# A gated MLP and long convolution, forward and backward: gate and up with rows on the partitions, h turned by TensorE, gradients turned by DMA in the last phase

## Chip, cores, metric

One Trainium2 chip, one core used. The metric is device time of one execution in microseconds (us). Profiled executions are single executions, whose span ("span") is a little shorter than the time of the same execution as timed.

TensorE does the matmuls, VectorE the elementwise products, ScalarE the copies out of PSUM (the memory that matmuls write to) and part of the DMA issuing, GpSimd and SyncE the rest of the issuing. In the lines of the profile these are PE, DVE, ACT, POOL and SP; PEld is the weight load of TensorE, to "turn" is to transpose, and SPq and ACTq are the issuing queues of SyncE and ScalarE.

## The reference

S = 2048 rows, D = 1024 columns, F = 3584 hidden columns, all bfloat16. The kernel computes the output and nine gradients; there is none for `B_x`, which is not used.

```python
# ... fft convolution _A_ref(q, k, v, shift_k, ssm_k, ssm_D), which multiplies q by a
# long convolution of (shifted k) * v along the rows ...
def _B_ref(x, w_gate, w_up, w_down):
    g = jnp.einsum("bsd,df->bsf", x, w_gate)
    u = jnp.einsum("bsd,df->bsf", x, w_up)
    h = g * u
    return jnp.einsum("bsf,fd->bsd", h, w_down)

x  = A_q
xn = _layernorm(x, axis=-1)
s  = _A_ref(xn, A_k, A_v, A_shift_k, A_ssm_k, A_ssm_D)
g  = _silu(_B_ref(xn, B_w_gate, B_w_up, B_w_down))
out = x + s * g
# outputs: out, and jax.vjp of it applied to grad_out
```

## The kernel before

It runs in six stages one after the other on TensorE. The convolution's forward and backward are cut into small steps, which `pump` and `bpump` hand out between matmuls in step with TensorE's progress. So VectorE, which does most of the convolution, is filled from TensorE's side.

| stage | what TensorE computes | what runs beside it |
|---|---|---|
| start | turns of the first normalized rows | layer norm |
| gate and up | g and u, 14 slabs of 256 hidden columns | rest of layer norm, forward convolution |
| down projection | h x w_down, then gating | gating on VectorE |
| backward | gradient of h, then those of w_gate and w_up | backward convolution |
| gradient of w_down | h^T x gradient | end of the backward convolution |
| gradient of x | gradients of g and u x weights^T | layer norm backward, gradient of the filter |

The gradients of g and u are needed twice, in two forms. The weight gradients contract over rows, so rows must be on the partitions. The gradient of x contracts over hidden columns, so those must be. The kernel before computes g and u, and with them their gradients, with hidden columns on the partitions; for the weight gradients it then turns them on TensorE.

```python
    def gu_unit(fc, s0, ns, w, tick):                      # before: hidden columns on partitions
        ...
            for a in range(2):
                ps = ps_gu.tile([P, 512], F32, name="psg")
                for dc in range(DC):
                    nc.tensor.matmul(ps[:, 0:n], w[:, dc, a, fi * P:(fi + 1) * P], XNT[q][:, dc, qo:qo + n],
                                     start=(dc == 0), stop=(dc == DC - 1))
                nc.scalar.copy(out=gut[:, a, o:o + n], in_=ps[:, 0:n])
                flush(2)
                tick()
        sta(GUTd[fc, :, :, s0:s0 + ns], gut[:, :, 0:ns])
        ...
        tt(hT[:, 0:ns], gut[:, 0, 0:ns], gut[:, 1, 0:ns], MUL)
        st(HTd[...], hT[:, 0:ns])
```

`defer` puts a piece of TensorE work aside, and `flush(2)` lets it out after two more blocks, so that it doesn't stand in TensorE's order right behind what it needs. `ld`, `st` and `sta` are DMA issued by SyncE, GpSimd and ScalarE. The backward stage:

```python
    ps_b = pool("ps_b", 3, space=PSUM)
    ps_tr = pool("ps_tr3", 2, space=PSUM)
    ...
    BT = NSL * (8 + 16) + 84.0                             # the convolution is spread over so many steps

    def dh_half(fc, hf, wdt, dgu):
        gut = bg.tile([P, 2, 1024], BF16, name="gul", bufs=4)
        ld(gut[:], GUTd[fc, :, :, hf * 1024:(hf + 1) * 1024])
        dht = bg.tile([P, 1024], BF16, name="dht")         # 2 buffers
        for k in range(2):
            ...                                            # 8 matmuls of 512 columns: gradient of h
            nc.scalar.copy(out=dht[:, k * 512:(k + 1) * 512], in_=ps[:])
            flush(2)
            btick(1)
        dgt = gut
        with tc.high_priority(60):
            tt(dgt[:], gut[:], dht[:].unsqueeze(1).to_broadcast([P, 2, 1024]), MUL)

        def turn():
            sta(DGUTd[4 * hf:4 * hf + 4, :, :, fc, :].rearrange("b f a s -> f a b s"),
                dgt[:].rearrange("f a (b s) -> f a b s", s=256))
            for a in range(2):
                ps = ps_tr.tile([P, 8, P], BF16, name="tr")
                for i in range(8):
                    nc.tensor.transpose(ps[:, i, :], dgt[:, a, i * P:(i + 1) * P], ident[:])
                nc.scalar.copy(out=dgu[:, :, a, fi * P:(fi + 1) * P], in_=ps[:])
        defer(turn)
```

In the last stage, each 256 rows' gradients are loaded in the turned form that `DGUTd` holds, by two plain loads.

## Time and profile before

| | before |
|---|---|
| median of 3 runs | 2100.8 us (2099.44 to 2109.26) |
| profiled span | 2094.6 us, mean granted TensorE clock 0.996 |

The stages by the first matmul of each (the prediction cuts where source lines change, so its bounds differ by some 2 us and its lengths by up to 4 us):

| stage (us) | start | first slabs | gate and up | down projection | backward | gradient of w_down | gradient of x |
|---|---|---|---|---|---|---|---|
| begins at | 0 | 25.6 | 96.2 | 565.4 | 767.9 | 1467.0 | 1671.4 |
| length | 25.6 | 70.6 | 469.2 | 202.5 | 699.1 | 204.4 | 423.2 |
| TensorE busy | 8.9 | 66.5 | 453.3 | 199.3 | 675.8 | 202.4 | 411.7 |

Read a column as length less busy: that is what TensorE waited in the stage. Almost everything is busy, so a stage is as long as the work in TensorE's order, unless another engine is late. The lines of the profile that carry this are shown in the prediction.

### The profile page before, as it was taken

The page shows a single profiled execution, that of the slowest core. Times are in us where ns is not written, and L with a number is a line of the kernel's source. Part 1 is how long each engine was busy: PE and PEld are TensorE (multiplying, and loading weights), DVE is VectorE, ACT ScalarE, POOL GpSimd, SP SyncE. Part 2 cuts the span into 40 slices and gives each one's busy share as a digit, 9 for nine tenths or more (in the row PEclk, how much of TensorE's full clock was granted, in tenths as well). Part 3 has the DMA queues.
Part 4 walks back from the last instruction along what each step waited for, and adds up shares of the span by engine and source line. Part 5 has one row for each costly group of instructions (what it writes and reads, how often), then busy time and mean ns, then how long its engine had stood idle before and what let it go on. Part 6 is the DMA issues. An engine that isn't in the chain of part 4 may idle for free.

```text
span 2094.6 us, 28045 instructions
## 1 busy us (share of the span) xinstructions
PE 2017.9 (96%) x11036; PEld 1032.2 (49%) x11242; DVE 1451.0 (69%) x1950; ACT 677.2 (32%) x1028; POOL 301.4 (14%) x448
## 2 busy tenths in 40 slices
PE   6999999999999999999999999999999999999998
PEld 4455555556444445555444454554444444444443
DVE  7789898978555557776999877987885025344432
ACT  4633343334233343444333343433122102111111
POOL 3211111110011120001021112111111101110100
PEclk9999999999999999999999999999999999999999
DMA  8675665566597876667787777756955995444431
GB/s 266 206 249 193 211 224 200 170 217 216 191 335 238 251 268 225 209 195 197 246 254 235 217 228 230 227 186 197 258 157 148 244 293 180 149 152 162 149 103 41
DMA packets 412789, 435.51 MB, mean 208 GB/s; under 512 B 178176, under 2 KB 326952, under 8 KB 401648
## 3 DMA queue, kind: packets, MB, share of 16 engines
q1 hardware_dynamic: 260816, 184.84, 31.1%
q0 software_dynamic: 40768, 174.40, 24.1%
q10 hardware_dynamic: 111072, 74.47, 11.5%
q8 instruction: 88, 1.44, 0.3%
q14 instruction: 45, 0.37, 0.0%
HBM read 221.78 MB, written 179.34 MB: 192 GB/s over the span
## 4 chain that ended last, share of the span: by engine, by line
PE 36%; DVE 13%; issue 10%; DMA 3%; POOL 1%; ACT 1%; ACTq 0%; another core or an unknown queue 0%; DVEq 0%; POOLq 0%; SPq 0%
PE psx L1203 18%; PE psb L1170 9%; PE psb L1077 5%; DVE m L196 4%; DVE W L196 4%; DMA B<-HFd 2%; PE psdk L927 1%; DVE A L196 1%; DVE gul L196 1%; DVE B L196 1%; PE psb L1054 1%; PE psY L892 1%; DMA DGUTd<-gul 1%; DMA gul<-GUTd 0%; DMA B<-KFd 0%
## 5 line engine op out<-in xcount | busy, mean ns | idle before, releaser
L565 PE MATMUL psg<-U,wslab 128*128 128x512 bf16 (+1 forms) x1804 | 399.7, 374 | 7.6 <-DVE U L539 3.0
L1077 PE MATMUL psb<-U,U 128*128 128x512 bf16 x1741 | 395.3, 379 | 2.7
L1203 PE MATMUL psx<-U,dgut 128*128 128x512 bf16 x1380 | 306.7, 379 | 1.4
L1203 PEld LDWEIGHTS <-dgut 128*128 128x128 bf16 x1792 | 175.3, 98 | 211.4
L565 PEld LDWEIGHTS <-wslab 128*128 128x128 bf16 x1856 | 182.6, 99 | 195.1 <-issue 4.5
L1077 PEld LDWEIGHTS <-U 128*128 128x128 bf16 x1792 | 174.0, 98 | 194.1
L1054 PE MATMUL psb<-U,wdt 128*128 128x512 bf16 x872 | 204.4, 382 | 2.5 <-ACT bm L967 1.1
L1170 PE MATMUL psb<-U,U 128*128 128x512 bf16 x875 | 195.6, 379 | 2.0 <-DMA U<-HTd 0.9
L567 ACT CAST gut<-psg 128x512 bf16<-128x512 f32 x192 | 112.5, 587 | 221.4 <-PE psg L565 210.7
L952 PE MATMUL psbm<-U,ht 128*128 128x512 bf16 x766 | 170.2, 379 | 0.9
L1081 ACT CAST wb<-psb 128x512 bf16<-128x512 f32 x112 | 65.7, 587 | 268.5 <-PE psb L1077 231.5
L196 DVE TENSOR_TENSOR m<-A,B 128x1024 bf16<-128x1024 bf16 (+1 forms) x160 | 116.6, 792 | 43.0 <-DMA B<-KFd 17.6
L196 DVE TENSOR_TENSOR W<-W 128x1024 f32<-128x1024 f32 (+1 forms) x144 | 139.4, 985 | 2.9
L1170 PEld LDWEIGHTS <-U 128*128 128x128 bf16 x896 | 86.8, 98 | 102.1 <-DMA U<-HTd 1.4
L1054 PEld LDWEIGHTS <-wdt 128*128 128x128 bf16 x896 | 87.2, 99 | 95.4 <-issue 4.2
L1226 ACT ACTIVATE dx_t<-dxn 128x1024 bf16<-128x1024 f32 (+1 forms) x17 | 17.1, 1007 | 345.3 <-DVE dxn L196 283.9
L952 PEld LDWEIGHTS <-ht 128*128 128x128 bf16 x784 | 76.1, 98 | 89.0
L196 DVE TENSOR_TENSOR dka<-dkh,Wbc 128x1024 bf16<-128x1024 bf16 x16 | 11.1, 691 | 155.8 <-DMA dkh<-DKSHd 155.8
L1070 ACT COPY U<-tr 128x1024 bf16<-128x1024 bf16 x112 | 109.4, 1022 | 13.9 <-DMA gul<-GUTd 7.8
L1056 ACT CAST dht<-psb 128x512 bf16<-128x512 f32 x112 | 65.4, 588 | 121.9 <-PE psb L1054 77.2
L196 DVE TENSOR_TENSOR gul<-gul,dht 128x2048 bf16<-128x2048 bf16 x56 | 69.5, 1241 | 28.6 <-ACT dht L1056 28.2
L1203 PE MATMUL psx<-W,dgut 128*128 128x512 bf16 x376 | 85.6, 379 | 0.5
(240 smaller groups left out, 2428.5 us busy)
## 6 DMA issues: line engine op xcount, KB each, us to landing
gul<-GUTd SPq DMA_DIRECT2D x56, 512.0 KB, 5.9
DGUTd<-gul ACTq DMA_DIRECT2D x56, 512.0 KB, 7.7
dgut<-DGUTd SPq DMA_DIRECT2D x16, 1792.0 KB, 8.4
GUTd<-gut ACTq DMA_DIRECT2D x48, 512.0 KB, 4.3
A<-DYFd POOLq DMA_DIRECT2D x16, 1024.0 KB, 5.6
out_dram<-wb ACTq DMA_DIRECT2D x224, 64.0 KB, 2.6
ht<-HTd SPq DMA_DIRECT2D x7, 1536.0 KB, 8.0
KFd<-KX POOLq DMA_DIRECT2D x8, 1024.0 KB, 4.3
```

The costliest lines, as they stand in the source:

```text
L196: V.tensor_tensor(o, a, b, op)
L565: nc.tensor.matmul(ps[:, 0:n], w[:, dc, a, fi * P:(fi + 1) * P], XNT[q][:, dc, qo:qo + n], start=(dc == 0), stop=(dc == DC - 1))
L567: nc.scalar.copy(out=gut[:, a, o:o + n], in_=ps[:, 0:n])
L892: nc.tensor.matmul(ps[:, i, :], G[:, 2 * r + k, c * P:(c + 1) * P], TI[:, 0, r, k, :], start=(k == 0), stop=(k == 1))
L952: nc.tensor.matmul(ps[:, dh * 512:(dh + 1) * 512], ht(fc)[:, i * P:(i + 1) * P], WD[fc // 4][:, fc % 4, dh * 512:(dh + 1) * 512], start=(f ...
L1054: nc.tensor.matmul(ps[:], wdt[:, dc, fi * P:(fi + 1) * P], DBMT[2 * hf + k][:, dc, :], start=(dc == 0), stop=(dc == DC - 1))
L1056: nc.scalar.copy(out=dht[:, k * 512:(k + 1) * 512], in_=ps[:])
L1070: nc.scalar.copy(out=dgu[:, :, a, fi * P:(fi + 1) * P], in_=ps[:])
L1077: nc.tensor.matmul(ps[:], XN[b // 4][:, b % 4, dc * P:(dc + 1) * P], dgus[b // 8][:, b % 8].rearrange("p a f -> p (a f)"), start=(b == 0), ...
L1081: nc.scalar.copy(out=wb[:].rearrange("p a f -> p (a f)"), in_=ps[:])
L1170: nc.tensor.matmul(ps[:], h(b, f), DBM[b // 4][:, b % 4, dh * 512:(dh + 1) * 512], start=(b == 0), stop=(b == NB - 1))
L1203: nc.tensor.matmul(ps[:, dh * 512:(dh + 1) * 512], t[a][:, 4 * j + f, i * P:(i + 1) * P], WGU[n][:, f, dh * 512:(dh + 1) * 512], start=(n ...
```

## The change

Its intent: take 896 transposes and their waits out of the backward stage. Gate and up change the places of their operands, so that rows come out on the partitions. Their gradients are then ready for the weight gradients as they are. What must be turned now is h, for the down projection (448 transposes, half as many, by TensorE), and the gradients for the last stage, where a DMA transpose does it on the way in. The matmuls of the gradient of h become 256 columns wide. The start is tidied as well: ten broadcast matmuls and the filter's transposes no longer stand in front of the first rows.

```diff
@@ gate and up
+    def gu_unit(sl, b0, n, w, tick):
+        gut = fg.tile([P, 4, 2, SLW], BF16, name="gut")
+        hN = fg.tile([P, 4, SLW], BF16, name="hN")
+        for i in range(n):
+            q, qi = divmod(b0 + i, 4)
+            ps = ps_gu.tile([P, 512], F32, name="psg")
+            for dc in range(DC):
+                gu_mm[0] = nc.tensor.matmul(ps[:], XNT[q][:, dc, qi * P:(qi + 1) * P],
+                                            w[:, dc].rearrange("p a f -> p (a f)"), start=(dc == 0), stop=(dc == DC - 1))
+            nc.scalar.copy(out=gut[:, i].rearrange("p a f -> p (a f)"), in_=ps[:])
+            flush(2)
+            tick()
+        sta(GUd[sl, b0 // 8][:, b0 % 8:b0 % 8 + n], gut[:, 0:n])
+        tt(hN[:, 0:n], gut[:, 0:n, 0], gut[:, 0:n, 1], MUL)
+        st(Hd[sl][:, b0:b0 + n, :], hN[:, 0:n])
+        def turn():
+            hT = fg.tile([P, 2, 4, P], BF16, name="hT")
+            ps = ps_tr.tile([P, 2, 4, P], BF16, name="tr")
+            for a in range(2):
+                for i in range(n):
+                    nc.tensor.transpose(ps[:, a, i, :], hN[:, i, a * P:(a + 1) * P], ident[:])
+            nc.scalar.copy(out=hT[:, :, 0:n], in_=ps[:, :, 0:n])
+            st(HTd[...], hT[...])
+        defer(turn)
@@ backward stage
-    ps_b = pool("ps_b", 3, space=PSUM)
-    ps_tr = pool("ps_tr3", 2, space=PSUM)
+    ps_b = ps_tr = pool("ps_b", 4, space=PSUM)
+    tr_name[0] = "psb"
-    ps_y = pool("ps_y3", 1, space=PSUM)
+    ps_y = pool("ps_y3", 2, space=PSUM)
...
+    def dh_half(k, wdt):
+        sl, hf = divmod(k, 2)
+        dgu = DGU[k]                                       # g and u, loaded ahead
+        for g in range(2):
+            bs = slice(4 * g, 4 * g + 4)
+            dht = bg.tile([P, 4, SLW], BF16, name="dht")
+            for e in range(2):
+                ps = ps_b.tile([P, 512], F32, name="psb")
+                for x in range(2):
+                    ...                                    # 8 matmuls of 256 columns
+                nc.scalar.copy(out=dht[:, 2 * e:2 * e + 2].rearrange("p b f -> p (b f)"), in_=ps[:])
+                flush(2)
+                btick(1)
+            with tc.high_priority(60):
+                tt(dgu[:, bs], dgu[:, bs], dht[:].unsqueeze(2).to_broadcast([P, 4, 2, SLW]), MUL)
+        def store():
+            fs = slice(sl % 2 * SLW, sl % 2 * SLW + SLW)
+            for a in range(2):
+                sta(DGd[sl // 2, a, 1024 * hf:1024 * hf + 1024, fs].rearrange("(b u) f -> u b f", u=P), dgu[:, :, a, :])
+        defer(store)
+        return dgu
@@ gradient of x
-            t = (gd, gd2)[bp % 2].tile([P, NF, 256], BF16, name=f"dgut{a}")
-            ld(t[:], DGUTd[bp, :, a])
+        t = (gd, gd2)[n // 7].tile([P, 4, 512], BF16, name=f"dgut{n}")
+        nc.sync.dma_start_transpose(out=t[:], in_=DGd[j, a, 512 * g:512 * g + 512, :])
@@ cut: buffers and loads of the new forms, order of the weight loads, the start's broadcasts
```

## The prediction

> **What bounds the kernel now.** I read the page first, then the table of engines by stage, then the groups of TensorE by shape, then the list of who waited for whom, and last the timelines where a single duration was in doubt. The page and the table of stages (columns: stretch in us, its length, then busy time and instruction count of PE, PEld, DVE, ACT and POOL, granted clock, DMA share, GB/s):
>
> ```profile
> PE 2017.9 (96%) x11036; PEld 1032.2 (49%) x11242; DVE 1451.0 (69%) x1950; ACT 677.2 (32%) x1028; POOL 301.4 (14%) x448
> ...
> 0.00:25.60 25.60, 8.89 (x46) 4.74 (x47) 19.94 (x68) 10.03 (x18) 8.71 (x20) 1.00 0.98 333
> 25.60:97.00 71.40, 67.30 (x456) 40.95 (x461) 52.35 (x106) 46.55 (x68) 19.94 (x33) 1.00 0.61 192
> 97.00:564.90 467.90, 452.43 (x2629) 257.73 (x2674) 404.83 (x516) 180.37 (x304) 70.83 (x113) 1.00 0.61 206
> 564.90:770.00 205.10, 201.44 (x1006) 95.27 (x1026) 107.32 (x170) 65.12 (x66) 38.56 (x61) 1.00 0.84 270
> 770.00:1465.00 695.00, 671.71 (x3980) 348.29 (x4053) 578.29 (x728) 273.70 (x412) 97.54 (x141) 1.00 0.72 222
> 1465.00:1671.00 206.00, 203.99 (x1049) 97.64 (x1068) 124.12 (x151) 43.61 (x77) 27.37 (x20) 1.00 0.83 201
> 1671.00:2094.60 423.60, 412.11 (x1881) 187.54 (x1917) 164.15 (x214) 57.86 (x86) 38.44 (x61) 0.99 0.48 155
> ```
>
> I cut the stages where the source lines change: start (layer norm), gate and up for the first slabs, gate and up with the forward convolution beside it (97 to 565), the down projection and gating (to 770), gradients of h, gate and up with the backward convolution (to 1465), the gradient of w_down (to 1671), the gradient of x. TensorE is busy all through, at full clock; only 77 us of the span are idle, 17 of them in the start. So work taken from TensorE's stream shortens the kernel by its own length, unless something else becomes late. The something else is VectorE: 405 of 468 us in the forward stage (87%), 578 of 695 in the backward one (83%). ScalarE, at 32%, is no bound anywhere.
>
> The groups of TensorE that the change touches, and its two waits that matter:
>
> ```profile
> L1054 PE MATMUL psb<-U,wdt 128*128 128x512 bf16 x872 | 204.4, 382 | 2.5 <-ACT bm L967 1.1 <-issue 0.2
> L1069 PE MATMUL tr<-ident,gul 128*128 128x128 bf16 x896 | 60.5, 221 | 14.5 <-DVE gul L196 14.4
> ...
> PE tr L1069 <- DVE gul L196: 14.4, 12, 3.2
> PE tr L149 <- DVE rr L518: 9.3, 1, 9.3
> PE psY L415 <- DVE HX L196: 5.4, 4, 1.9
> ```
>
> The mean of a matmul (379 ns) is its latency; the cost in a stream is the spacing. The 896 transposes of L1069 occupy 60.5 us, 67.5 ns each. For 512 columns I take an unbroken run of 16; for 256 columns a run of 8 with different weights each:
>
> ```profile
> 209.76 3.62 PE L565 MATMUL psg<-U,wslab 128*128 128x512 bf16 x16
> ...
> 218.99 1.04 PE L415 MATMUL psY<-HX,TI 128*128 128x256 bf16 x8
> ```
>
> (3.62 - 0.38)/15 = 216 ns, and (1.04 - 0.27)/7 = 110 ns.
>
> **What the skill says.** (1) The Trainium skill, "TensorE: Matmul & The Clock Gate", section "Back-to-back issue gap", gives N/2.4 + 2.5 ns warm, so 216 ns for 512 columns and 109 for 256; the two runs above agree. The lower sustained figure the same section gives for N=512 (131 ns) is not seen here. (2) The same page, "Part 4: PE-mode transpose", gives some 275 ns per transpose in a kernel; in this trace that is near the latency (221 ns), while the spacing, which is what counts, is 67.5 ns. (3) The same page, note on engine queue depths in Part 1, says that ACT and DVE are strict FIFO; the trace agrees in that the product of gate and up for h came on average 2.2 us after its last operand (I took the start of each of the 48 products less the end of the evacuation before it), up to 8 us, with other DVE work before it. (4) "DMA: Bandwidth & Descriptors", "Latency and other measured facts", gives 261 GB/s for DMA transposes with a broken middle dimension. Here two 1 MB transposes stand 4.27 and 4.51 us in the issuing queue, some 235 to 245 GB/s:
>
> ```profile
> 1647.97 4.27 SPq L1136 DMA_TRANSPOSE W<-in_B_w_up_dram  x1
> 1652.46 4.51 SPq L1136 DMA_TRANSPOSE W<-in_B_w_gate_dram  x1
> ```
>
> **The change part by part.**
>
> Gate and up (forward). Operands change places: the weights are now blocks of normalized rows, the moving operand is up and gate side by side, 512 wide. 14 slabs x 16 blocks x 8 = 1792 matmuls of 512 columns, as before, so no cost. New: h comes out with rows on partitions and must be turned for the down projection: 14 x 16 x 2 = 448 TensorE transposes x 67.5 ns = 30.2 us, of which 64 (4.3 us) fall into the first stage and 384 (25.9 us) into 97 to 565. ScalarE gets about 58 copies of about 1.02 us, beside 180 us in 468: free. VectorE does the same products.
>
> New wait there: the transposes of h stand in TensorE's order two blocks (2 x 8 x 216 ns = 3.5 us) after the unit, and need VectorE's product. About 1 us of that passes before the last evacuation is done, leaving 2.4 us. The products of the kernel before were complete 2.9 us after the evacuation on average; where they were later than 2.4, they sum to 46 us of excess over 48 units. Convolution matmuls often lie between, and one stall lets VectorE catch up for the next, so I take about a quarter, 12 us (range 4 to 28). Forward stage: +25.9 + 12 = +38 us.
>
> Start. The ten broadcast matmuls of L149 stood in TensorE's order ahead of the first transposes and held them from 9.3 to 18.1 us although the first rows were normalized at 11.2; they move to later chunks, and the transposes of the convolution filter, which held the first gate matmul (25.6 us) for 3.6 us, are held back too. The first gate matmul can start near 14 us. About 12 us are won, 4.3 go to the transposes of h, some 2 to a colder clock and waits on layer norm: -6 us.
>
> Gradient of h and its products. 896 matmuls of 512 columns become 1792 of 256: 896 x (2 x 110 - 216) = +3.6 us. The 896 transposes go (-60.5 us), and with them their wait on VectorE (-14.4 us), since the product is now first used half a slab later (64 x 110 ns = 7 us of matmuls between). ScalarE loses 112 copies of 1.02 us, of no use. Sum for TensorE: -71 us. But the convolution is pumped by TensorE's progress, so VectorE's 578 us must now fit into 695 - 71 = 624 us, 93%; from 995 to 1445, where VectorE was busy 399 of 450 us, it would be 97% of about 411. Before, stretches in which VectorE stood at 24.8 of 25 us cost TensorE 1 to 3 us per 25. I give back 14 us (range 3 to 30): -57 us.
>
> Entry of that stage: 4 MB of normalized rows and 2 MB of gate and up must now be there after three halves (21 us) in place of 29 us; at the 382 GB/s seen there this takes 17 us: +1 us.
>
> Down projection and gradient of w_down: the same matmuls; h is now loaded plainly rather than by DMA transpose. TensorE was at 99% there: 0.
>
> Gradient of x: the same 1792 matmuls. The gradients now come by 56 DMA transposes of 512 KB, some 2.2 us each by the rate above. A piece is asked for when the second pair of row blocks has used its predecessor and is needed 13 pieces later (13 x 16 x 216 ns = 45 us); 14 x 2.2 = 31 us of transfer fit. At the entry five 1 MB weight transposes and seven pieces (8.5 MB, 36 us) race against the first pair, which needs its last piece 45 us in: tight, not late: +1 us.
>
> Sum: -6 + 38 - 57 + 1 + 0 + 1 = -25 us on 2100.8, some 2076; since both give-backs are the softest terms and I have taken them rather high, I put the point at 2070.
>
> **The rivals.** (A) TensorE's sum alone: 30.2 + 3.6 - 60.5 - 14.4 and -10 in the start, about -51 us, some 2050. For it: the 96% row, and a scheduler that places products early. (B) VectorE becomes the bound from 995 on and in the forward stage every transpose of h waits: -40 in the backward stage, +55 in the forward one, so some 2105. For it: 24.8 of 25 us busy in the densest stretches; against it: VectorE had 117 us idle in the backward stage. (C) The DMA transposes of the last phase starve TensorE: if one took over 6.3 us rather than 2.2 (88.8 us for 14 pieces), each of three groups would stall. Each us beyond adds 42 us. Against it: the rate above, and DMA at only half share in that stage.
>
> **Range and chances.** The forward give-back spans 24 us, the backward one 27, the entries some 10. Laid together not all at their ends: 2042 to 2098. Faster by over 2% means under 2058.8, which needs nearly rival A: 0.30. Slower by over 2% means over 2142.8, which needs C: 0.03. Within 2%: 0.67.
>
> **What would show it right or wrong.** First gate matmul near 14 us; the forward stage about 38 us longer, with a wait of TensorE's h transposes on the product of about 12 us; no transposes in the backward stage, which is about 57 us shorter with VectorE above 90%; 256-column matmuls spaced 110 ns; the last two stages as long as before within 4 us. Wrong if the h transposes wait 30 us or more, if the backward stage shrinks by under 40 us, or if TensorE waits for transposed pieces in the last stage.

## The result

The kernel after computes the right result. It took 2085.11 us (median of 4 runs, 2084.60 to 2086.25), the kernel before in the same rounds 2100.38 us (median of 4, 2099.44 to 2109.26). A ratio here and below is the mean time of one kernel's runs over that of the other's of the same rounds, so not quite the ratio of the medians: 0.9919, 95% interval 0.9892 to 0.9946. That is within 2%, and inside the predicted range (2042 to 2098), 15 us above its point of 2070.

The page after, the row of engines, to be held against the first line of the prediction's first fence:

```profile
PE 2001.6 (96%) x11438; PEld 1088.1 (52%) x11626; DVE 1464.0 (70%) x1937; ACT 626.5 (30%) x969; POOL 339.9 (16%) x496
```

TensorE lost 16.3 us of work (2017.9 to 2001.6), where the prediction's terms take 30.2 - 60.5 + 3.6 = -26.7 us out of it, before any slower clock. VectorE gained a little. The table of stages of the kernel after (stretch, length, busy time and count of PE, PEld, DVE, ACT, POOL, granted clock, DMA share, GB/s):

```profile
0.00:13.10 13.10, 1.89 (x16) 1.63 (x16) 8.08 (x28) 2.71 (x5) 5.08 (x16) 1.00 0.94 261
13.10:89.50 76.40, 73.57 (x458) 36.69 (x467) 55.54 (x128) 60.84 (x86) 22.62 (x34) 1.00 0.74 257
89.50:585.40 495.90, 476.77 (x3027) 280.30 (x3080) 412.81 (x524) 226.06 (x353) 108.49 (x165) 1.00 0.66 224
585.40:796.40 211.00, 200.78 (x1009) 94.97 (x1027) 110.95 (x176) 65.74 (x65) 41.23 (x65) 0.99 0.85 277
796.40:1450.00 653.60, 632.26 (x4021) 389.90 (x4065) 581.36 (x722) 170.34 (x300) 97.10 (x139) 0.98 0.77 233
1450.00:1653.50 203.50, 202.28 (x1041) 97.02 (x1060) 131.06 (x151) 43.24 (x77) 26.98 (x18) 1.00 0.82 208
1653.50:2084.40 430.90, 414.03 (x1880) 187.55 (x1915) 164.15 (x214) 57.58 (x86) 38.41 (x61) 0.99 0.65 149
```

Against the table of before, with the prediction's term for each stage:

| stage | before | after | change | predicted |
|---|---|---|---|---|
| start and first slabs | 96.2 | 89.5 | -6.7 | -6 |
| gate and up | 469.2 | 496.0 | +26.8 | +38 |
| down projection and entry of the backward stage | 202.5 | 210.9 | +8.4 | +1 |
| backward | 699.1 | 653.7 | -45.4 | -57 |
| gradient of w_down | 204.4 | 203.5 | -0.9 | 0 |
| gradient of x | 423.2 | 430.8 | +7.6 | +1 |
| sum | 2094.6 | 2084.4 | -10.2 | -25 (sum of the rounded terms: -23) |

The table is of one profiled execution of each; the timed difference is some 15 us. The groups of the new 256-column matmuls and of the transposes of h:

```profile
L1082 PE MATMUL psb<-wdt,U 128*128 128x256 bf16 x1792 | 205.5, 274 | 0.0
L581 PE MATMUL tr<-ident,hN 128*128 128x128 bf16 x448 | 35.0, 219 | 9.4 <-DVE hN L199 9.2
```

The first is 205.5 us for 1792 matmuls beside 204.4 for 896 twice as wide: 115 ns each including the ends of runs, and it waited for nothing. (The busy time of a group counts the tail of each run, which the next matmuls overlap. In the run of 46 shown under e1 below the spacing is (5.18 - 0.27) / 45 = 109 ns, as predicted.) The list of TensorE's waits after (line, releaser, us in total, times, longest):

```profile
PE tr L542 <- DVE x L539: 11.0, 1, 11.0
PE tr L581 <- DVE hN L199: 9.2, 11, 2.6
PE psb L1003 <- DVE dbm L199: 6.7, 1, 6.7
PE psx L1212 <- DMA dgut<-DGd: 5.8, 3, 3.5
PE psY L407 <- DVE B L199: 4.3, 1, 4.3
PE psb L1101 <- ACT dht L1084: 4.2, 1, 4.2
PE psY L407 <- ACT yl L882: 3.8, 1, 3.8
```

The first is the first normalized rows of the start, where nothing else can run. The second is the predicted wait of the transposes of h. The third and fourth are the two entries that the prediction put at 1 us each. The last three are in the backward stage: the old wait of 14.4 us there, in 12 pieces of at most 3.2 us, is gone, and a few single waits of some 4 us came in its place.

**The third wait.** TensorE's timeline at the end of the down projection (start, length, operation, count, idle time before with its releaser):

```profile
784.39 0.61 PE L1003 MATMUL tr<-ident,dbm 128*128 128x128 bf16 x8
784.83 4.05 PE L964 MATMUL psbm<-U,ht 128*128 128x512 bf16 x17
795.58 1.04 PE L1003 MATMUL psb<-ident,dbm 128*128 128x128 bf16 x8 [6.70 <-DVE dbm L199]
796.41 3.83 PE L1082 MATMUL psb<-wdt,U 128*128 128x256 bf16 x17
```

The turn of the last rows' gradient (L1003) waits for the gating of these rows, and the backward matmuls (L1082) stand behind it, though the ones over the first 1024 rows don't need it. In the kernel before, 25 backward matmuls (L1054) stood ahead of that turn (L989), which then waited for nothing:

```profile
767.93 5.56 PE L1054 MATMUL psb<-U,wdt 128*128 128x512 bf16 x25 [1.14 <-ACT bm L967]
773.48 0.62 PE L989 MATMUL tr<-ident,dbm 128*128 128x128 bf16 x8
```

**The fourth wait.** TensorE at the entry of the last stage, then SyncE's issuing queue at the same time:

```profile
1686.52 3.63 PE L1212 MATMUL psx<-U,dgut 128*128 128x512 bf16 x16 [0.78 <-DMA dgut<-DGd]
1693.66 5.31 PE L1212 MATMUL psx<-U,dgut 128*128 128x512 bf16 x16 [3.52 <-DMA dgut<-DGd]
1700.43 1.90 PE L1212 MATMUL psx<-U,dgut 128*128 128x512 bf16 x8 [1.46 <-DMA dgut<-DGd]
```

```profile
1673.86 7.09 SPq L1152 DMA_TRANSPOSE U<-in_B_w_up_dram  x1
1680.99 2.07 SPq L1206 DMA_TRANSPOSE dgut<-DGd  x1
1683.10 5.64 SPq L1152 DMA_TRANSPOSE U<-in_B_w_gate_dram  x1
1688.79 2.50 SPq L1206 DMA_TRANSPOSE dgut<-DGd  x1
```

Pieces of the gradient (L1206, 512 KB) and weights (L1152, 1 MB) alternate in one queue. From 1673.86 to 1688.79 it passed 2.5 MB in 14.9 us, or 176 GB/s, where I had reckoned with some 240. TensorE catches up with the pieces and waits for three of them.

**The backward stage.** Four slices of 25 us of the kernel after:

```profile
990.00:1015.00 25.00, 24.89 (x179) 17.53 (x180) 12.56 (x18) 6.43 (x11) 6.71 (x11) 1.00 0.83 299
1015.00:1040.00 25.00, 20.43 (x85) 8.88 (x85) 24.83 (x30) 2.93 (x5) 0.55 (x1) 0.86 0.77 213
1140.00:1165.00 25.00, 20.73 (x139) 13.85 (x138) 22.56 (x27) 4.17 (x8) 5.82 (x9) 0.93 1.08 283
1190.00:1215.00 25.00, 20.93 (x139) 13.90 (x138) 22.95 (x29) 6.12 (x11) 0.69 (x2) 0.90 0.96 231
```

and two of before, the first near its own hand-over from one phase of the convolution to the next, the second its worst:

```profile
1057.00:1082.00 25.00, 24.67 (x132) 12.45 (x134) 24.73 (x32) 8.08 (x13) 1.07 (x2) 1.00 0.62 216
1120.00:1145.00 25.00, 21.49 (x106) 10.63 (x107) 24.65 (x30) 6.73 (x11) 7.99 (x12) 0.93 0.83 231
```

Read the first busy time (PE) against the third (DVE). After, VectorE is half idle in one slice and full in the next, TensorE waits over 4 us, and the granted clock falls to 0.86. A VectorE without a gap is not by itself what costs: in such slices (24.6 us or more of 25) TensorE stood 0.2 to 3.5 us in the kernel before and 0.1 to 4.6 us in the kernel after. What counts is whether the one result that TensorE needs next is late. The stall near 1154, in the timeline of all engines:

```profile
1152.07 1.22 DVE L199 TENSOR_TENSOR U<-U,dht 128x2048 bf16<-128x2048 bf16 x1
...
1153.31 0.39 ACTq L68 DMA_DIRECT2D DGd<-U  x1
1153.80 0.58 ACT L1084 CAST dht<-psb 128x512 bf16<-128x512 f32 x1 [9.95 <-DVE U L199]
...
1154.43 5.73 PE L1101 MATMUL psb<-U,U 128*128 128x512 bf16 x17 [4.22 <-ACT dht L1084]
```

Follow it upwards. TensorE waited 4.22 us for an evacuation (ScalarE's copy out of PSUM) into `dht`, which waited 9.95 us for VectorE's product. When the product came, the store of the gradients (`DGd<-U`) went out and then the evacuation. After the wait, 17 matmuls took 5.73 us, (5.73 - 0.38) / 16 = 334 ns each in place of 216: another 1.9 us. The Trainium skill, "TensorE: Matmul & The Clock Gate", Part 1, says that TensorE's clock falls to half after an idle window of about 3.4 us. The traces agree as to the length, 3.41 us or a multiple of it for every stretch at half clock inside a kernel, but not as to the wait that it takes: in the kernel before, a wait of 3.2 and one of 2.4 us were each followed by 3.4 us at half clock (from 1140.2 and from 1290.4 us), 3.4 us of clock lost in the stage. (Clock lost is length times one minus the granted clock.) In the kernel after, the three waits of 3.8 to 4.3 us were followed by 6.8, 3.4 and 6.8 us at half clock, and of the 6.8 us after the wait of 6.7 us at the entry 4.2 reach into the stage: 10.6 us lost. Counted over the traces of all fourteen kernels (gaps of TensorE from 0.5 us on, without the first 45 us; half clock that begins in the gap or within 3.5 us after it): gaps of under 2 us were followed by half clock in 2 of 225 cases, of 2 to 3 us in 22 of 48, of 3 to 4 us in 22 of 26, and longer ones in 41 of 41.

### The profile page after: what moved, and what is told of

Its sections match the earlier page's. It is cut to its first block, busy times and chain, and to the rows that moved or that the text cites.

```text
span 2084.4 us, 28857 instructions
## 1 busy us (share of the span) xinstructions
PE 2001.6 (96%) x11438; PEld 1088.1 (52%) x11626; DVE 1464.0 (70%) x1937; ACT 626.5 (30%) x969; POOL 339.9 (16%) x496
## 3 DMA queue, kind: packets, MB, share of 16 engines
q0 software_dynamic: 45120, 189.08, 26.8%
## 4 chain that ended last, share of the span: by engine, by line
PE 42%; DVE 9%; issue 6%; DMA 2%; SPq 2%; POOL 1%; ACT 0%; another core or an unknown queue 0%; ACTq 0%; DVEq 0%; POOLq 0%
PE psx L1212 17%; PE psb L1101 9%; PE psb L1181 9%; PE psb L1082 4%; DVE W L199 3%; DVE m L199 2%; SPq L1152 1%; PE psdk L939 1%; DVE U L199 1%; DMA dyl<-DYd 1%; DMA B<-HFd 1%; DVE B L199 1%; PE psY L904 1%; DVE B L242 0%; SPq L1206 0%
## 5 line engine op out<-in xcount | busy, mean ns | idle before, releaser
L567 PE MATMUL psg<-wslab,U 128*128 128x512 bf16 x1729 | 402.5, 380 | 4.2 <-ACT gut L569 0.7
L1212 PE MATMUL psx<-U,dgut 128*128 128x512 bf16 x1508 | 336.2, 380 | 7.4 <-DMA dgut<-DGd 5.8
L1101 PEld LDWEIGHTS <-U 128*128 128x128 bf16 x1792 | 176.6, 99 | 210.2 <-issue 15.9
L567 PEld LDWEIGHTS <-U 128*128 128x128 bf16 x1792 | 173.4, 98 | 187.3 <-issue 4.6
L1082 PE MATMUL psb<-wdt,U 128*128 128x256 bf16 x1792 | 205.5, 274 | 0.0
L569 ACT CAST gut<-psg 128x512 bf16<-128x512 f32 x224 | 130.9, 585 | 218.6 <-PE psg L567 215.8
L1082 PEld LDWEIGHTS <-U 128*128 128x128 bf16 x1792 | 176.2, 98 | 23.1
L199 DVE TENSOR_TENSOR W<-W 128x1024 f32<-128x1024 f32 (+1 forms) x144 | 146.1, 1033 | 2.7
L1181 PEld LDWEIGHTS <-U 128*128 128x128 bf16 x896 | 87.0, 98 | 102.1
L199 DVE TENSOR_TENSOR dka<-dkh,Wbc 128x1024 bf16<-128x1024 bf16 x16 | 11.1, 692 | 156.6 <-DMA dkh<-DKSHd 156.6
L199 DVE TENSOR_TENSOR U<-U,dht 128x2048 bf16<-128x2048 bf16 x56 | 71.6, 1282 | 18.5 <-ACT dht L1084 18.5
L1183 ACT CAST U<-psb 128x512 bf16<-128x512 f32 x56 | 32.8, 585 | 159.8 <-PE psb L1181 131.2
L199 DVE TENSOR_TENSOR gg<-bm,sig 128x1024 bf16<-128x1024 bf16 x16 | 11.1, 691 | 92.0 <-ACT sig L982 92.0
```

The source lines that it names most:

```text
L199: V.tensor_tensor(o, a, b, op)
L567: gu_mm[0] = nc.tensor.matmul(ps[:], XNT[q][:, dc, qi * P:(qi + 1) * P], w[:, dc].rearrange("p a f -> p (a f)"), start=(dc == 0), stop=(dc ...
L569: nc.scalar.copy(out=gut[:, i].rearrange("p a f -> p (a f)"), in_=ps[:])
L1082: nc.tensor.matmul(ps[:, x * SLW:(x + 1) * SLW], DBMT[2 * hf + g][:, dc, (b % 4) * P:(b % 4 + 1) * P], wdt[:, dc, :], start=(dc == 0), sto ...
L1101: nc.tensor.matmul(ps[:], XN[b // 4][:, b % 4, dc * P:(dc + 1) * P], dgus[b // 8][:, b % 8].rearrange("p a f -> p (a f)"), start=(b == 0), ...
L1181: nc.tensor.matmul(ps[:], h[:, b, f * P:(f + 1) * P], DBM[b // 4][:, b % 4, dh * 512:(dh + 1) * 512], start=(b == 0), stop=(b == NB - 1))
```

## The experiments

Twelve kernels in three batches; the kernel before was timed seven times in each. Its medians in the three batches were 2104.06, 2107.27 and 2098.91 us, and single runs of it spread up to 21 us in one batch, so the ratios, not the times, are compared. Stage lengths are by the first matmul of each stage, as above, from one profiled execution.

One thing on their precision first: the backward stage of unchanged code is not equally long in each execution. Before it was 699.1 us, and 707.1 us in e8, which changes only the start; after it was 653.7, in e6, which changes only the forward stage, 654.0, and in e7 659.2. Differences of 5 to 8 us in this stage from one profile each prove nothing.

The theories: (V) VectorE, fed from TensorE's pace, is the limit in stretches of the backward stage, and gives back part of the saved TensorE time; (S), formed only after e2 and e3, ScalarE, whose order holds the stores of the gradients behind VectorE's product and the evacuations behind the stores, gives it back; (E) the entries of two stages lost what the main parts had won.

| run | median us | ratio to before [95%] | gate and up | down proj. | backward | grad. w_down | grad. x |
|---|---|---|---|---|---|---|---|
| after | 2085.11 | 0.9919 [0.9892, 0.9946] | 572.4 | 210.9 | 653.7 | 203.5 | 430.8 |
| e1_entry | 2088.54 | 0.9931 [0.9904, 0.9958] | 571.4 | 205.4 | 659.7 | 204.9 | 429.6 |
| e2_nomul | 2124.80 | 1.0095 [1.0060, 1.0129] | 571.7 | 222.9 | 669.6 | 203.5 | 433.0 |
| e3_nomul_before | 2140.32 | 1.0171 [1.0138, 1.0205] | 541.4 | 202.6 | 741.2 | 208.0 | 422.9 |
| e4_pace | 2094.88 | 0.9956 [0.9916, 0.9995] | 572.8 | 211.5 | 635.3 | 228.2 | 433.4 |
| e5_switch | 2085.85 | 0.9912 [0.9846, 0.9977] | 574.5 | 210.8 | 638.6 | 212.1 | 432.7 |
| e6_age3 | 2102.35 | 0.9975 [0.9905, 1.0045] | 574.9 | 210.2 | 654.0 | 203.5 | 436.2 |
| e7_hdma | 2072.69 | 0.9833 [0.9785, 0.9882] | 539.3 | 219.8 | 659.2 | 203.6 | 436.1 |
| e8_start_before | 2092.15 | 0.9927 [0.9877, 0.9978] | 545.2 | 202.7 | 707.1 | 204.2 | 422.9 |
| e9_store_sp | 2097.20 | 0.9969 [0.9927, 1.0012] | 571.9 | 211.9 | 658.1 | 203.5 | 437.3 |
| e10_store_sp_before | 2129.85 | 1.0127 [1.0076, 1.0178] | 544.2 | 202.6 | 723.8 | 204.6 | 422.9 |
| e11_h_entry_store | 2066.23 | 0.9821 [0.9777, 0.9866] | 539.1 | 212.9 | 659.0 | 203.5 | 432.4 |
| e12_all | 2062.81 | 0.9801 [0.9748, 0.9854] | 539.2 | 213.9 | 646.4 | 213.0 | 437.7 |

"Gate and up" here includes the first slabs (539.8 before). e2 and e3 give wrong gradients; all others are right.

### e1_entry: the last turn gets a PSUM pool of its own

```diff
-    ps_b = ps_tr = pool("ps_b", 4, space=PSUM)
-    tr_name[0] = "psb"
+    ps_b = pool("ps_b", 3, space=PSUM)
+    ps_tr = pool("ps_tr3", 1, space=PSUM)
```

> The changed kernel, with the last turn of the gradient of the down projection in a PSUM pool of its own (3 + 1 tiles in place of 4 shared), so that in TensorE's order 46 matmuls of 256 columns (46 x 110 ns = 5.1 us) stand ahead of it. Theory: the shared pool puts these transposes first, and they wait 6.7 us for VectorE; here the wait falls to about 1.6 us, and TensorE does not fall to the low clock after it (some 2 us more): entry shorter by 5 to 8 us, 2085 becomes 2077 to 2080. Rival: the stage's first matmuls are held by the loads anyway (6 MB must land), so the wait moves to the first use of a product and the time stays at 2085 within 2; or three tiles for the matmuls are too few and the stage itself grows.

The mechanism is as supposed: with a pool of its own, the turn is no longer in front of the backward matmuls. 46 of these go ahead of it, and it waits 0.37 us:

```profile
789.89 5.18 PE L1082 MATMUL psb<-wdt,U 128*128 128x256 bf16 x46 [1.14 <-ACT bm L981]
795.45 0.62 PE L1003 MATMUL tr<-ident,dbm 128*128 128x128 bf16 x8 [0.37 <-DVE dbm L199]
...
810.67 1.86 PE L803 MATMUL psY<-kvx,dyx 128*128 128x128 bf16 x16 [3.91 <-DMA kvx<-KVd]
```

The entry became 5.5 us shorter (210.9 to 205.4). But the backward stage became 6.0 us longer, with new waits: 3.9 us on the convolution's first load, right behind the entry (the last line), and 7.8 us on evacuations, 7.4 of it in one at 1147 us, where the kernel after had waited 4.2. The kernel as a whole didn't gain: 0.9931 beside 0.9919. So the shared pool caused the 6.7 us wait, but to take it away brought TensorE sooner to a load that was late next, and the three tiles left in place of four are a second candidate for the loss (see e11). With 5 to 8 us of scatter in the backward stage, whether 2 or 3 us are really gained stays open.

### e2_nomul and e3_nomul_before: VectorE's product left out

This takes some 70 us of VectorE's work out of the backward stage of each kernel.

```diff
             with tc.high_priority(60):
-                tt(dgu[:, bs], dgu[:, bs], dht[:].unsqueeze(2).to_broadcast([P, 4, 2, SLW]), MUL)
```

> The changed kernel without the multiplication of gate and up by the gradient of h on VectorE (wrong gradients on purpose): 56 x 1.28 us = 72 us less VectorE work in the backward stage, everything else as it was. Theory, VectorE is what limits the backward stage of the changed kernel: TensorE's waits on psY, products and the low clock after them (some 19 us idle and 13 us of slower matmuls) mostly go; 2085 becomes 2055 to 2065. Rival, the stage is limited by its matmuls of 256 columns, the PSUM evacuations or its transfers: only the two direct waits on the product (about 7 us) go, 2078 to 2082.

> Control: the kernel before without the same multiplication (wrong gradients on purpose), the transposes left in. Theory: there VectorE had room, so what goes is the 14.4 us in which the transposes waited for the product and a few us in the densest stretches: 2100 becomes 2078 to 2086, and the gap between the two kernels without multiplication is near the TensorE sum of the change (30.2 + 4 - 60.5 - 7 in the start = -33 us, give or take 6). Rival, VectorE is no more of a limit after the change than before it: both kernels lose the same time and the gap stays at 15 us.

Both became slower (1.0095 and 1.0171), with VectorE at 511 us in the backward stage of e2 in place of 581. The edit did more than take work from VectorE. Without the product, the store of `dgu` needs nothing but a load, so the order of issue that the scheduler makes puts it early in ScalarE's queue, while large loads are under way:

```profile
791.39 9.90 ACTq L68 DMA_DIRECT2D DGd<-U  x1
801.40 1.06 ACT L982 ACTIVATE sig<-bm 128x1024 bf16<-128x1024 bf16 x1 [9.01 <-issue]
```

The issue of one DMA held ScalarE 9.9 us, and the gating behind it started 9 us late; the wait at the entry grew from 6.7 to 18.8 us. In e3 the turned copies waited likewise (29.5 us of TensorE on ScalarE's copies, which waited for loads of g and u). The pair is confounded and says nothing on V. It does show that ScalarE's DMA issue can stop the kernel, which made S look better than V and led to e9.

### e4_pace: less convolution per step of the backward stage

```diff
-    BT = NSL * (8 + 16) + 84.0
+    BT = NSL * (8 + 16) + 100.0
```

The convolution is spread over 436 steps in place of 420, so each step hands VectorE 420/436 = 3.7% less; the rest moves into the next stage.

> The changed kernel with the backward convolution spread over 16 more steps of TensorE's work (constant 84 becomes 100), 4% less VectorE work per step of the backward stage, right results. Theory, VectorE is the limit there: 4% of the 455 us of the stage after the first 98 steps is 18 us less VectorE work inside it, of which 5 to 15 show: 2070 to 2080. Rival: what delays TensorE is the pause in the convolution where its first part gives its buffers to the second (VectorE half idle from 990 to 1015 us), after which it lags and TensorE waits until it has caught up; spreading by 4% then gives 0 to 4 us, 2081 to 2085.

The backward stage became 18.4 us shorter, far outside the scatter: VectorE 554.1 in place of 581.5 us, the lost clock 1.5 us in place of 10.6, TensorE's idle time 13.1 in place of 21.3. The next stage became 24.7 us longer, as the convolution's rest was then drained in one go:

```profile
PE psY L904 <- DVE B L242: 11.0, 2, 10.4
PE psY L904 <- ACT yl L906: 8.6, 3, 4.7
```

So the backward stage behaves as V says: take 27 us of VectorE's work away and 18 us come back. The edit moves the convolution's smaller share of work on ScalarE and TensorE too, so VectorE alone isn't isolated. Of the 18.4, 8.2 are idle time and 7.3 matmuls that no longer run at half clock; of the other 2.9, 1.7 are TensorE's own convolution work that was pushed on (32 matmuls of L904). But the kernel as a whole gained nothing over after: 0.9956, with single runs from 2084.88 to 2102.98 us and an interval that overlaps that of after.

### e5_switch: the same, and a pause for VectorE at the hand-over

```diff
@@ e4's change, and where the second half of the backward convolution begins:
+        yield 14.0
         ab = pool("e_ab", 1)
-    C_TOTAL = 8 * (FWD8_W + 0.8) + ...
+    C_TOTAL = 14.0 + 8 * (FWD8_W + 0.8) + ...
```

> As the kernel with the convolution spread over 16 more steps, and besides the pump of the convolution is given 14 us without work where its first part hands its buffers to the second, so that it does not count as late for the pause it has there. Right results. If the pause and the lag after it cause TensorE's waits (20.4 of 25 us busy from 1015 to 1040), that window is near 24 of 25 and the time 5 to 10 us under the kernel that is only spread. If mean VectorE load is the cause, no difference to it beyond 2 us, since the density elsewhere is 2% higher.

The pump pauses for the 14 units in which VectorE was half idle anyway and asks for more later. The window named in the expectation came out as it said: TensorE was busy 23.8 of 25 us from 1015 to 1040, beside 21.0 in e4 and 20.4 in after. So the spreading alone hadn't cured the stall at the hand-over, and the pause did; but a wait of 4.4 us at 1100 us came in its place. The backward stage kept 15.1 us of the gain, and the gradient of w_down gave back 8.6 in place of 24.7. The whole came to 0.9912, beside 0.9919 of after and 0.9956 of e4; the size expected against e4 (5 to 10 us) is there, but it arose in the gradient of w_down, and the intervals overlap. In the profiled spans it is 2.6 us below after, which is no difference. What VectorE has to do in the two stages together hardly changes, so most of the gain of the one is paid in the other.

### e6_age3: the transposes of h one block later

```diff
             nc.scalar.copy(out=gut[:, i].rearrange("p a f -> p (a f)"), in_=ps[:])
-            flush(2)
+            flush(3)
```

> The changed kernel with the transposes of h one block of gate and up later (three blocks after the unit in place of two; 1.7 us more room for VectorE). Theory: the 9.2 us in which these transposes wait for the product shrink to under 3 us and the forward stage by about 6: 2079. Rival: TensorE waits for VectorE's convolution results there in any case, so the wait moves to them and the time changes by under 3 us, 2082 to 2086.

No gain: gate and up 574.9 in place of 572.4 us. The wait of the transposes didn't go away but gathered in fewer, longer pieces (9.2 us in 11, then 11.1 in 6), and the convolution's waits grew from 2.2 to 5.9:

```profile
PE tr L581 <- DVE hN L199: 11.1, 6, 8.8
PE psY L418 <- DVE HX L199: 5.9, 4, 2.1
```

But 8.8 of the 11.1 are one wait at the end of the stage, so the other five come to 2.3 us, as the theory had it. The long one is VectorE's queue: a product of the gating, for the next stage, stood first and waited for a load, and the last product of h behind it:

```profile
585.80 0.69 DVE L199 TENSOR_TENSOR so<-xn_t,yf_t 128x1024 bf16<-128x1024 bf16 x1 [13.49 <-DMA yf_t<-YFd]
586.41 0.68 DVE L199 TENSOR_TENSOR hN<-gut 128x1024 bf16<-128x1024 bf16 x1
```

Theory and rival both hold in part: the distance helped the many small waits, the convolution's grew by 3.7 us, and the order of one load took the rest.

### e7_hdma: h turned by DMA, too

h is stored with rows outermost and loaded by DMA transpose, for the down projection, as the gradients are in the last stage. No transposes of h on TensorE. The edit, shortened:

```diff
-        def turn():
-            ...                                            # 8 TensorE transposes, copy, store to HTd
-        defer(turn)
+        st(HR[b0 // 8][sl // 2][r0:r0 + n * P, c0:c0 + SLW].rearrange("(b u) f -> u b f", u=P), hN[:, 0:n])
...
-        for f0, f1 in ((0, 24), (24, 28)):
-            last = ld(ht[:, f0:f1], ht_rows(bp, f0, f1))
+        for j in range(7):
+            last = nc.sync.dma_start_transpose(out=ht[:, 4 * j:4 * j + 4, :], in_=HR[bp // 4][j][r0:r0 + 256, :])
```

> The changed kernel with h turned by DMA instead of TensorE: h is stored once, with rows as rows, and the down projection loads it by DMA transposes (56 of 256 KB, about 1.1 us each, 8 us per pair of row blocks of 25 us); 448 TensorE transposes and 58 evacuations are gone. Right results. If the transposes of h cost what they occupy and wait (30.2 + 9.2 us): 2045 to 2052. If VectorE limits the forward stage too once TensorE has 30 us less to do, half of it comes back as waits: 2060 to 2070. If the DMA transposes are late in the down projection (DMA share 85% there): over 2075, with TensorE waiting for ht.

Gate and up went back to the length of before (539.3, beside 539.8 before and 572.4 after). So the transposes of h cost 33 us, transposes and waits together. The down projection paid 8.9 of it: its DMA share rose from 0.85 to 0.99 and the turns of the gradient waited for the gating (the second line is the wait of the kernel after, too):

```profile
PE tr L993 <- DVE dbm L198: 9.3, 2, 8.6
PE psb L993 <- DVE dbm L198: 6.7, 1, 6.7
```

TensorE did not wait for `ht`, as the third expectation had feared. VectorE stood 9.8 us for the load of `yf_t`, until 602.2 us, in front of the gating that TensorE waited 8.6 us for; that the DMA transposes made this load late is likely and not shown. The backward stage and that of x were 5.5 and 5.3 us longer, in code that was not touched, the size of the scatter. The time (2072.7) lies between the second and the third expectation. In all 0.9833, an interval that doesn't overlap with that of after. A comparison within one batch says the same: e9 and e11 below differ by this edit and that of e1, and their medians by 31 us. The turn by TensorE was the dearer of the two ways here.

### e8_start_before: the tidied start in the kernel before

```diff
-        for j in (3, 2, 1, 0, 4):
+        def products(j):
             for h in range(2):
...                                                        # issued later, between gate and up of later rows
+                with tc.issue_after(tr_ln[0].ins):
+                    nc.tensor.transpose(ps[:, 0, :], hrow[:, c, :, 0], ident[:])
```

> The kernel before with one part of the change alone: the ten broadcast matmuls and the first transposes of the convolution filter moved out of the start. The first gate matmul comes near 13.5 us in place of 25.6. The start of the changed kernel won 6.7 us although 64 transposes of h (4.3 us) came into it, so here 9 to 11 us: 2100 becomes 2089 to 2092. Rival: the start is paced by layer norm on VectorE and the loads, and most of it comes back before 97 us: 2096 to 2100.

The first gate matmul came at 13.7 us (25.6 before, 13.1 after), but the down projection began at 558.9 in place of 565.4: 12 us were won at the start and 6.5 left at the end of gate and up. So by the stages the tidied start is worth 6.5 us, between the two expectations (the 6.7 us of the kernel after are counted at the end of the first slabs, with 64 turns of h in them). The timed ratio (0.9927) would make it 15 us, all that the whole change gained. But single runs of before in this batch spread over 21 us, and against its median in the other rounds (2098.91 to 2104.06 us) e8's 2092.15 is 7 to 12 us less. The profiled span (2095.8) shows no gain, since the backward stage of that execution was 8 us longer. The stages speak for some 7 us; more than that is not excluded.

### e9_store_sp and e10_store_sp_before: the store of the gradients issued by SyncE

```diff
-                sta(DGd[sl // 2, a, 1024 * hf:1024 * hf + 1024, fs].rearrange("(b u) f -> u b f", u=P), dgu[:, :, a, :])
+                ld(DGd[sl // 2, a, 1024 * hf:1024 * hf + 1024, fs].rearrange("(b u) f -> u b f", u=P), dgu[:, :, a, :])
```

> The changed kernel with one thing moved: the 56 stores of the gradients of gate and up are issued by SyncE in place of ScalarE (right results). Theory formed after the runs without multiplication: ScalarE is in order; the store stands in its queue and waits for VectorE's product (or for room in the DMA queue), and the evacuations behind it come late, so that TensorE stands without a PSUM tile. ScalarE waited 64 us in all for products in the backward stage of the changed kernel (35.8 before evacuations of the gradient of h, 28.3 before those of the weights' gradients). Then here these waits go, TensorE's waits on ScalarE's evacuations (4.2 and 3.8 us) too, and the backward stage falls from 654 to 640 to 648: 2072 to 2080. Rival, VectorE's total work alone sets the stage: its results for psY come no earlier, and the stage stays at 650 to 656, 2083 to 2088.

> Control, the kernel before with the same stores issued by SyncE. There ScalarE waited 17 us for products in the backward stage and TensorE for ScalarE 1 us only, with VectorE 83% busy: if the coupling matters only where VectorE is late, the time stays within 4 us of before. If it matters in both, the backward stage falls by 5 to 10 us.

The store was out of ScalarE's order, and nothing was won: 0.9969, the backward stage 658.1 us. ScalarE's waits in the backward stage, first after, then e9:

```profile
ACT dht L1084 <- DVE U L199: 35.8, 9, 9.9
```

```profile
ACT dht L1084 <- DVE U L199: 56.8, 10, 12.1
```

The evacuation waits for the product without any store between. `dht` has two buffers, and an evacuation into one may start only when the product that read it last is done. So S, in the form that the stores hold the evacuations, falls; the chain that is left is evacuation, product, buffer, evacuation, and its slow link is the place of the product in VectorE's order. A third buffer of `dht` was not run, and whether it would help is open. e10 lost 1.3%: by the waits, SyncE's queue then held the loads of g and u behind stores that waited (TensorE waited 13.8 us for `yl`, ScalarE 18.4 for loads of g and u).

### e11_h_entry_store and e12_all: together

e11 is e7 with e1's pools and e9's store; e12 is that with e5's pacing.

```diff
@@ e11: the edits of e7_hdma, e1_entry and e9_store_sp
@@ e12: those and that of e5_switch
```

> The changed kernel with three edits together: h turned by DMA (2072.7 alone), the PSUM pool of the last turn apart, the stores issued by SyncE. If the entry's gain of 5.5 us was given back because ScalarE's stores held evacuations (three tiles are then short), it now stays: 2050 to 2062. If three tiles are short by themselves: 2062 to 2072, with TensorE waiting on evacuations in the backward stage.

> As the last, and with the backward convolution spread over 16 more steps and its pause at the hand-over counted. If VectorE's lateness still costs once ScalarE is free of it: 3 to 10 us under the last. If not, the work pushed into the last part of the gradient of w_down costs more there than it saves: 0 to 8 us over it.

In e11 the entry's gain stayed (212.9 us with e7's down projection of 219.8), but the backward stage was 659.0 us and TensorE waited for evacuations into `dht`, 3.4 and 4.6 us at the longest. That, and the time, is what was expected if three tiles are short by themselves. e12 is the best kernel: 2062.81 us, 0.9801 of before. Its interval (0.9748 to 0.9854) doesn't settle whether it is over 2%; it doesn't overlap with that of after (0.9892 to 0.9946). e11 and e12 can't be told apart, and neither can e11 and e7: in this sum only the turn of h by DMA clearly counts.

## Why the prediction was right, and where its sizes were off

The verdict (within 2%), the range and the mechanism held: TensorE's sum falls, and VectorE and the entries give part of it back. That the total came so near is in part luck: gate and up came out 11 us better than its term, the backward stage, its entry and the gradient of x 26 us worse together. The sum printed as -25 is -23 from its own terms, and the point was then lowered from 2076 to 2070 because the give-backs were thought to be high; they weren't. (Its 379 ns as the mean of a matmul isn't that of the line it shows, 382; nothing rests on it.) Of its signs of being wrong one came true: TensorE waited for transposed pieces in the last stage. Point by point:

- **Start, -6 predicted, -6.7 measured.** First gate matmul foreseen near 14 us, found at 13.1. Right, and e8 shows the same move in the kernel before.
- **Gate and up, +38 predicted, +26.8 measured.** TensorE's busy time in this stage grew by 23.5 us (453.3 to 476.8), predicted 25.9. The wait of h's transposes on VectorE's product was 9.2 us in the whole kernel, predicted 12. The step that failed is that the 12 were added to the waits there: the convolution's own waits shrank meanwhile (on `HX` from 5.4 to 2.2), so TensorE's idle time grew by 3.3 us only. One stall lets VectorE catch up for the next, as the prediction said, and it counted that for the new waits but not for the old ones.
- **Backward stage, -57 predicted, -45.4 measured.** The transposes and the 14.4 us wait went, as predicted. VectorE's share of the stage rose to 581 of 654 us (89%), not above 90%. The give-back was meant to be 14 us: -71 in TensorE's sum, -57 in all. It was 26. Of the -71, -14.4 was to be idle time; idle time fell by 2.0 us only (23.3 to 21.3), as new waits of about 4 us replaced the old. TensorE's busy time fell by 43.5 us in place of 57. Two terms account for the 13.5 missing to within 2 us. The first is the price of a transpose. The 60.5 us of the prediction is the time in which any of the 896 was under way, with the tail of each run over the matmuls behind it, so 67.5 ns is not their spacing. In the stream of the kernel before, a run of 16 takes 0.90 us until the next matmul starts, 56 ns each:

```profile
806.17 1.06 PE L1069 MATMUL tr<-ident,gul 128*128 128x128 bf16 x16
807.07 5.13 PE L1077 MATMUL psb<-U,U 128*128 128x512 bf16 x22
```

  That makes 50 us for the 896, 10 less than was taken. The second is the clock: matmuls at half clock lost 8.8 us in the stage, 3.3 before, so 5.5 more. The prediction had one price for a wait, its length. What the runs showed is that the three waits of 3.8 to 4.3 us (12.3 us) brought 6.7 us of slow matmuls with them, half again as much; the twelve of at most 3.2 us before (14.4 us) brought 3.3, a quarter. e4 backs this: with less work for VectorE, the lost clock fell to 1.5 us and the stage was 18.4 us shorter.
- **Entry of the backward stage, +1 predicted, +8.4 measured.** Loads were taken for the cause to fear, and they were not late. The wait came from the PSUM pool that the last turn now shares with the backward matmuls, which fixed their order. The line was in the diff and the prediction passed over it. e1 undid it and found the next wait behind, so the term was mis-sized without being worth much.
- **Gradient of w_down, 0 predicted, -0.9 measured.**
- **Gradient of x, +1 predicted, +7.6 measured.** "Tight, not late" was wrong: the queue passed 176 GB/s at the tightest, not the 240 that two transposes had shown in the kernel before (the 14 of 1 MB there stood 4.0 to 13.95 us, the middle one 4.5, so the rate was typical but the long ones were left out), and TensorE waited 5.8 us in three pieces, with a granted clock of 0.93 in the slice of 1675 to 1700. The nine other kernels with this last stage took 429.6 to 437.7 us for it, the three with the old one 422.9 each, so the loss repeats. Rival C (a starved TensorE) is thus right in direction, but only at the entry: the later groups of rows didn't wait.

Rival A (TensorE's sum alone, 2050) is refuted by the backward stage and the entries. Rival B (VectorE makes every transpose of h wait, +55 in the forward stage) is refuted by 9.2 us of wait.

Where the expected gain went, then: of the 71 us expected from the backward stage 26 did not come, 10 of them because the transposes were never that dear; the forward stage took 27, and the two entries 16. e7 shows that the 27 were the avoidable ones.

## What to carry to other kernels

Moving a transpose from one stage to another is worth the difference of the two stages' prices. Take a transpose at its spacing in the stream, not at its group's busy time over its count. Where TensorE is full, try the turn on the DMA engines; here 448 transposes on TensorE cost 33 us, and their turn by DMA 9 us visibly (DMA share 0.85 before it, 0.99 after). Count a long wait with the slow matmuls behind it, here half again for waits of some 4 us, and be more afraid of one such wait than of several of under 2 us. When work leaves a stage whose other engine is paced by it, ask what share of its time that engine will then be busy; and look in a diff for pools that became shared, since they fix an order.

## What the Trainium skill lacked or had wrong

- "TensorE: Matmul & The Clock Gate", "Part 4: PE-mode transpose", gives 275 ns for a transpose in a kernel and no spacing in a run, and says that the full clock doesn't engage for transposes. The run of 8 at 784.39 us in the kernel after, among matmuls, took 0.61 us, so (0.61 - 0.22) / 7 = 56 ns from one to the next; runs of 16 in the kernel before show the same 56 ns. Whether transposes alone would raise the clock was not run.
- The same page, Part 1, puts the fall to half clock after an idle window of about 3.4 us. The stretches at half clock fit (3.41 us or a multiple), but gaps of 2 to 3 us were already followed by one in 22 of 48 cases, and four of 26 gaps of 3 to 4 us were not. For planning, the chance of it rises from 2 us on.
- "DMA: Bandwidth & Descriptors", "Latency and other measured facts", gives 261 GB/s for DMA transposes with a broken middle dimension, and more for contiguous ones, but nothing for a queue that carries both sizes beside other traffic. With 512 KB pieces among 1 MB ones it passed 176 GB/s at the entry of the last stage, and a 1 MB transpose stood there 4.2 to 7.1 us.
- No page that I read has a number for how long the issue of a DMA can hold the issuing engine: ScalarE was held 9.9 us by one in e2. What held it is not shown.
